# Keys of the first scores in two halves, zero products in every gap of the opening, and new places for three turns

## The chip, the cores and the metric

One core of one Trainium2 chip runs the whole program. The metric is device time in microseconds (us) of one execution, the median of several runs.

## The reference, cut to what matters

```python
B, H, S, D = 4, 8, 768, 48
f = 1.0 / (1.0 + np.exp(-f_logit))
for t in range(S):
    state = f[:, :, t, :, None] * state + np.einsum('bhd,bhe->bhde', k[:, :, t], v[:, :, t])
    y[:, :, t] = np.einsum('bhd,bhde->bhe', q[:, :, t], state)
x = y.transpose(0, 2, 1, 3).reshape(B * S, H * D)          # 3072 x 384
h = x @ w_in                                               # 384 -> 2048
g = np.where(h >= 1, h, np.where(h <= -1, 0.0, (h + 1) ** 2 / 4))
out = g @ w_out                                            # 2048 -> 384
```

All of it is float32. A linear attention with a gate for each head and channel gives the tokens of a two-layer network.

## The kernel before, in words

**Tiling.** The 768 tokens are cut into six steps of 128 (`NI`, `C`). In a step the eight heads are taken in four pairs (`PAIRS`, `NP`), and a pair's operands hold all four batches side by side, 4 x 128 = 512 columns (`N`): keys in the first 512 columns of its tile `kq`, queries in the next 512. Pair 3 of a step is made of rows that are left over from the three tiles of 16 + 96 channels into which the 384 channels of the network are cut; in step 0 it is loaded on its own, in later steps its keys and queries are moved out of the tiles of pairs 0 to 2 (`move`, L295, six small transfers a step). A pair is numbered through all steps, so pair 3 of step 0 is 3, pairs 4 to 7 are those of step 1. In the trace the four tiles are one name, `kq`; in the order of the program kq_67 to kq_70 belong to pairs 0 to 3.

**Step 0, the opening.** For each pair `first_loads` (L444) issues the gate logits (192 KB) and the keys and queries (512 KB) on SP's queue, by `dma` (L292), pair 3 first. ScalarE (ACT) makes log(1 + exp(-logit)) of them in two passes (L455, L456). `first_gates` (L458) sums these over time on TensorE (PE), one product with a triangle of ones for each batch (L465); ACT takes the exponentials of the sums, of either sign (L468, L469), and VectorE (DVE) multiplies keys and queries by them in place (L473, L474). `scores` (L564) are sixteen records of products of keys with queries, L572 (two heads by four batches), masked by DVE (L579, L585). `last_heads` (L808) and `half_tile` (L820) multiply the masked scores with the values (L806) for the tiles of the network's input: "last" is pair 3's share, "heads" of a tile its own pairs' share, and "tile" the products that put pair 3's rows into the tile (L836). Whichever of "heads" and "tile" comes first for a tile opens its bank in PSUM; where that is "heads", a product with zeros clears the bank first (L827). `unit_0` (L853) is the first product with w_in.

**Behind it.** The network runs in 96 units: a step has 16 slices of w_in, w_out (`NJ`). A unit's nine products of x with w_in (L266) are followed by ACT and DVE (L269 to L280) and by nine products with w_out for the unit before (L287). The parts of w_in, w_out are split into high and low halves while they arrive (`split_piece`, lines 362 to 373). Between the units stand the attention's blocks of the next steps: the table `TURNS` (L57) says at which unit a pair is prepared and its keys transposed ("turn", L640, with L642's copies behind it), `VISITS` (L58) at which units two pairs' scores, states and outputs are made. `prepare` issues the pair's loads, gates and moves too.

**What sets the order.** Every operation is given to `Plan` with an engine, a cost in ns (`COST`) and what it needs. TensorE's operations keep the order in which they are added: `START` (L59) for the opening, then the units with their tables. For the other engines and the queues `Plan.order` (L116) runs the list against its own costs and sets one order for each engine, by what is free, ready and due. The program is then written out in that order; it is fixed, and each instruction waits for semaphores of what it needs. A DMA issue on SP that waits holds back all that stand behind it.

**Zero products.** `warm_first` (L335, tuple `WARM`, L61) gives PE 32 products with zeros before the first operands are there. Later, the loop that writes the program out (L1001) puts products of 512 columns with zeros (`warm`, L329, L332) where the plan shows a gap on PE: from 7 to 20 us, gaps over 350 ns, and behind 20 us, those over 500 ns.

## Time and profile before

| | |
|---|---|
| median of three runs | 469.04 us (468.89 to 469.52) |
| the profiled execution | 469.33 us |
| its span in the trace | 467.5 us |
| PE busy in the span | 460.9 us, 99% |
| DVE busy | 346.5 us, 74% |
| ACT busy | 299.4 us, 64% |
| mean traffic | 106 GB/s of HBM over the span |

All times in the trace count from the start of the span; the execution is 1.8 us longer than its span. L12 is line 12 of the kernel. Engines that run beside PE cost nothing as long as PE has work, so a share is read together with the chain of work that ended last and, in a stretch, with the engine's timeline and what released each wait. PE is TensorE's products, PEld its weight loads, POOL is GpSimd, SP the queue that issues nearly all transfers.

### The profile page before, as it was taken

What the parts mean: (1) busy time and instruction counts of PE and PEld (TensorE: products, weight loads), DVE (VectorE), ACT (ScalarE), POOL (GpSimd) and SP (SyncE); (2) the same over time, 40 slices, a digit from 0 to 9 for tenths busy, and PEclk for the clock granted to TensorE, in tenths of its full rate; (3) what the DMA queues carried; (4) which work ended last, traced back from release to release, by engine and by line L of the source; (5) the groups of instructions that cost most, each with busy time, mean ns of one, the idle gap of its engine ahead of it and who ended that gap; (6) DMA issues with size and microseconds to landing.
All of it is one profiled execution on the core that took longest, in us unless ns stands there. A gap on an engine that the chain in (4) does not pass through costs nothing.

```text
span 467.5 us, 11025 instructions
## 1 busy us (share of the span) xinstructions
PE 460.9 (99%) x4525; PEld 378.8 (81%) x4525; DVE 346.5 (74%) x689; ACT 299.4 (64%) x551; POOL 22.6 (5%) x75
## 2 busy tenths in 40 slices
PE   8999999999999999999999999999999999999996
PEld 7887788888888888888888888888888888888884
DVE  2989998789999889989878788566766755533332
ACT  7798998989566776578475546654545454644443
POOL 2202010000000200000020001000000000000000
PEclk9999999999999999999999999999999999999999
DMA  8878685444023333053335323245322224300001
GB/s 271 310 241 257 187 285 181 169 129 145 1 69 126 105 78 102 2 193 109 75 84 193 129 67 91 68 130 127 126 81 70 67 79 126 102 1 0 1 0 71
DMA packets 21861, 54.36 MB, mean 116 GB/s; under 512 B 3568, under 2 KB 4464, under 8 KB 21808
## 3 DMA queue, kind: packets, MB, share of 16 engines
q1 hardware_dynamic: 21664, 53.57, 37.0%
q8 instruction: 36, 0.59, 0.6%
q14 instruction: 17, 0.14, 0.1%
q10 hardware_dynamic: 144, 0.07, 0.1%
HBM read 44.96 MB, written 4.72 MB: 106 GB/s over the span
## 4 chain that ended last, share of the span: by engine, by line
PE 92%; DVE 3%; ACT 2%; DMA 1%; issue 1%; SPq 0%; DVEq 0%; ACTq 0%
PE po L287 41%; PE ph L266 39%; PE pa L688 2%; PE pa L710 2%; PE ph L621 1%; DVE kn L655 1%; DMA raw<-in_l 1%; PE pa L759 1%; PE po L572 1%; PE pa L806 1%; DVE glo L280 1%; PE pa L640 1%; PE ph L860 0%; DVE act L277 0%; PE pa L621 0%
## 5 line engine op out<-in xcount | busy, mean ns | idle before, releaser
L266 PE MATMUL ph<-x,w_hi 128*128 128x512 f32 x570 | 146.5, 389 | 0.0
L269 ACT ACTIVATE act<-ph,half 128x512 f32<-128x512 f32 x96 | 66.1, 689 | 93.2 <-PE ph L266 92.8
L266 PEld LDWEIGHTS ph<-x,w_hi 128*128 128x128 f32 x570 | 106.8, 188 | 22.6 <-ACT w_hi L372 0.4
L277 DVE SCALAR_TENSOR_TENSOR act<-ph,act 128x512 f32<-128x512 f32 x96 | 66.2, 690 | 61.6 <-ACT act L272 60.5
L889 ACT CAST ghi<-act 128x512 fp32r<-128x512 f32 x96 | 59.4, 619 | 51.1 <-DVE act L277 50.5
L287 PE MATMUL po<-ghi,w_hi 128*128 128x512 f32 x288 | 86.3, 401 | 0.0
L287 PE MATMUL po<-ghi,w_lo 128*128 128x512 f32 x288 | 83.2, 390 | 0.0
L287 PE MATMUL po<-glo,w_hi 128*128 128x512 f32 x288 | 82.9, 389 | 0.0
L280 DVE TENSOR_TENSOR glo<-act,ghi 128x512 fp32r<-128x512 f32 x96 | 66.2, 689 | 21.5 <-ACT ghi L889 20.0
L266 PE MATMUL ph<-x,w_lo 128*128 128x512 f32 x285 | 81.7, 389 | 0.0
L655 DVE STREAM_TRANSPOSE kn<-kq 32x128 f32<-32x128 f32 x224 | 67.7, 302 | 3.6
L287 PEld LDWEIGHTS po<-ghi,w_lo 128*128 128x128 f32 x288 | 54.1, 188 | 11.6
L287 PEld LDWEIGHTS po<-glo,w_hi 128*128 128x128 f32 x288 | 54.1, 188 | 11.5
L266 PEld LDWEIGHTS ph<-x,w_lo 128*128 128x128 f32 x285 | 53.5, 188 | 11.1
L272 ACT ACTIVATE act<-act 128x512 f32<-128x512 f32 x96 | 60.7, 632 | 2.9
L287 PEld LDWEIGHTS po<-ghi,w_hi 128*128 128x128 f32 x288 | 51.9, 188 | 11.3 <-ACT ghi L889 0.3
L383 DVE TENSOR_REDUCE ok<-raw 128x1 f32<-128x384 f32 x64 | 33.2, 545 | 2.2 <-DMA raw<-in_w 2.2
L367 ACT ACTIVATE bits<-raw,top_of 128x384 uint32<-128x384 fp8e4 x32 | 20.1, 642 | 1.1 <-DMA raw<-in_w 1.1
L558 ACT ACTIVATE sd<-sd,kq 112x48 f32<-112x48 f32 x80 | 19.2, 324 | 0.0
L373 DVE TENSOR_TENSOR w_lo<-bits,w_hi 128x384 fp32r<-128x384 f32 x32 | 17.6, 554 | 1.9 <-ACT w_hi L372 1.7
L503 DVE TENSOR_TENSOR_SCAN w<-rec,f 128x512 f32<-128x512 f32 x15 | 18.3, 1220 | 0.9 <-ACT f L502 0.8
L369 DVE SCALAR_TENSOR_TENSOR bits<-raw,bits 128x384 uint32<-128x384 uint32 x32 | 17.4, 550 | 0.0
(137 smaller groups left out, 372.5 us busy)
## 6 DMA issues: line engine op xcount, KB each, us to landing
raw<-in_w SPq DMA_DIRECT2D x32, 384.0 KB, 3.1
raw<-in_w SPq DMA_DIRECT2D x32, 383.6 KB, 3.8
kq<-in_kq SPq DMA_DIRECT2D x15, 512.0 KB, 5.0
v<-in_v SPq DMA_DIRECT2D x12, 384.0 KB, 4.6
out_y<-raw SPq DMA_DIRECT2D x18, 256.0 KB, 2.7
f<-in_f SPq DMA_DIRECT2D x15, 256.5 KB, 3.3
kq<-in_k SPq DMA_DIRECT2D x4, 512.0 KB, 7.2
kq<-kq SPq DMA_DIRECT2D x30, 64.2 KB, 3.5
```

Source lines behind the costliest of these rows:

```text
L266: nc.tensor.matmul(ps, w_in(w_hi if high else w_lo, j, kt), xt[:, kt, t], start=(n == 0), stop=(n == 8))
L269: nc.scalar.activation(a, ps, AF.Relu, bias=half, scale=0.5)
L272: nc.scalar.activation(a, a, AF.Square)
L277: nc.vector.scalar_tensor_tensor(out=a, in0=ps, scalar=1.0, in1=a, op0=ALU.max, op1=ALU.min)
L280: nc.vector.tensor_tensor(out=lo, in0=a, in1=hi.bitcast(F32), op=ALU.subtract)
L287: nc.tensor.matmul(po[e], w_out(part, j, e), g, start=(j == 0 and n == 0), stop=(j == NJ - 1 and n == 2))
L367: m = sca("bits", lambda: nc.scalar.activation(t, top, AF.Abs, bias=top_of, scale=2.0 ** 30), loaded, made[k - 4] if k >= 4 else None, set ...
L383: seen.append(vec("join", lambda z=z, op=op: nc.vector.tensor_reduce(out=ok[:, 1 + NG + z + c:2 + NG + z + c], in_=words_of(raw[2])[1].bit ...
L503: s1 = vec("scan", lambda: nc.vector.tensor_tensor_scan(out=wide(w), data0=wide(rec), data1=ft[:, N:0:-1], initial=0.0, op0=ALU.mult, op1= ...
L558: nc.scalar.activation(ds[:, at + b * D:at + (b + 1) * D], state[:, p * B + b], AF.Copy, scale=pf[:R, b:b + 1])
L655: nc.vector.transpose(kn[n % 2][to:to + 32, ::-1, r:r + 32], src[:, :, u:u + 32])
L889: o = g["hi"] = sca("copy", lambda: nc.scalar.copy(hi, a), o, unit_out.get(u - 2))
```

## The change

- The gates and scores of pair 3 in step 0 are made in two halves of two batches: logits, logarithms, sums, exponentials, multiplies and scores each in two (numbers 3 and 7 in `START`).
- The logits of the second half are issued on ACT's queue. Pair 3's keys and queries come in two transfers of 256 KB: the inner columns 256 to 767 (the keys of batches 1 and 0, which lie last, and the queries of batches 0 and 1), then the outer quarters, columns 0 to 255 and 768 to 1023.
- `START` has another order: pair 2's gates go ahead of pair 1's, and for each tile "tile" goes ahead of "heads", for tile 0 too, so that no bank is cleared.
- `WARM` is seven products of 512 columns and two of 256. A new function, `fill`, puts zero products of 256 columns into every planned gap of over 100 ns between 4 and 20 us.
- The planner's figures for the opening's transfers (`KB_FIRST`, `KB_LATER`, `KB_L`) and halves are new, and with them the order of SP, ACT and DVE.
- `TURNS` puts the turns of pairs 5 to 9, 18, 19, 22 and 23 earlier (by one unit, those of 8 and 9 by four). `VISITS` puts the three visits of pairs 4 and 5 one unit earlier, the outputs of pairs 8 and 9 and the three visits of pairs 10 and 11 one unit later.

```diff
+KB_FIRST, KB_LATER, KB_L = 1.75, 0.82, 1.0
+COST = dict(half_gates=460, half_scores=570, half_log=330, half_sig=330, half_gate=350, gates=870,
...
-TURNS = {4: 4, 5: 5, 6: 9, 7: 9, 8: 19, 9: 19, 10: 25, 11: 25, 12: 28, 13: 28, 14: 37, 15: 37, 16: 40, 17: 40, 18: 47, 19: 47, 20: 61, 21: 61, 22: 70, 23: 70}
-VISITS = {4: (5, 6, 7), 6: (10, 12, 13), 8: (21, 22, 25), 10: (25, 26, 28), 12: (28, 32, 37), 14: (37, 39, 40), 16: (40, 46, 47), 18: (47, 60, 61), 20: (61, 69, 70), 22: (70, 75, 77)}
-START = (("gates", 3), ("gates", 0), ("scores", 3), ("mask", 3), ("gates", 1), ("scores", 0), ("mask", 0), ("gates", 2), ("last", 3),
-         ("scores", 1), ("mask", 1), ("heads", 0), ("scores", 2), ("mask", 2), ("tile", 2), ("tile", 1), ("tile", 0), ("heads", 1), ("heads", 2), ("unit", 0), ("unit", 1), ("unit", 2))
-WARM = 28 * (128,) + 4 * (256,)
+TURNS = {4: 4, 5: 4, 6: 8, 7: 8, 8: 15, 9: 15, 10: 25, 11: 25, 12: 28, 13: 28, 14: 37, 15: 37, 16: 40, 17: 40, 18: 46, 19: 46, 20: 61, 21: 61, 22: 69, 23: 69}
+VISITS = {4: (4, 5, 6), 6: (10, 12, 13), 8: (21, 22, 26), 10: (26, 27, 29), 12: (28, 32, 37), 14: (37, 39, 40), 16: (40, 46, 47), 18: (47, 60, 61), 20: (61, 69, 70), 22: (70, 75, 77)}
+START = (("gates", 3), ("gates", 7), ("gates", 0), ("scores", 3), ("scores", 7), ("mask", 3), ("gates", 2), ("gates", 1), ("last", 3),
+         ("scores", 0), ("scores", 1), ("mask", 0), ("tile", 0), ("heads", 0), ("scores", 2), ("mask", 1), ("tile", 1), ("heads", 1), ("mask", 2), ("tile", 2), ("heads", 2), ("unit", 0), ("unit", 1), ("unit", 2))
+WARM = 7 * (512,) + 2 * (256,)
 BY_PRODUCT, ON_EITHER = (), 16
 AFTER = {0: (("turn", 0), ("turn", 1)), 1: (("states", 0),), 2: (("turn", 2), ("turn", 3)), 3: (("states", 2),)}
...
                 nc.tensor.matmul(opened["bank"], zeros, zeros.rearrange("p (o c) -> p o c", o=1).broadcast_to([128, 4, 128]),
                                  start=opened["start"], stop=opened["start"])
+    def fill(gap):
+        for _ in range(int(gap / 115 + 0.5)):
+            nc.tensor.matmul(ph[1][:, 0:256], zeros, zeros.rearrange("p (o c) -> p o c", o=1).broadcast_to([128, 2, 128]), start=True, stop=True)
+
     def warm_first():
         for cols in WARM:
             nc.tensor.matmul(ph[1][:, 0:cols], zeros, zeros[:, 0:128].rearrange("p (o c) -> p o c", o=1).broadcast_to([128, max(cols // 128, 1), 128])[:, :, 0:min(cols, 128)], start=True, stop=True)
...
     cleared = add("POOL", 500, clear)
+    def later_half(n):
+        ends = [a.rearrange("r (o z) -> r o z", o=4)[:, 0:4:3] for a in (kq[n][:, 0:2 * N], kd[n])]
+        return dma(*ends, KB_FIRST * 256)
+
     def first_loads(n):
         c, a = att[n], LOGS[n]
+        raw_l = WEIGHTS[n][1][:, 0:BOTH]
+        c["l"] = []
+        parts = 2 if n == NP - 1 else 1
+        some = [slice(k * B // parts, (k + 1) * B // parts) for k in range(parts)]
+        loads = []
+        for k in range(parts):
+            cols = slice(k * BOTH // parts, (k + 1) * BOTH // parts)
+            if k == 0:
+                loads.append(dma(raw_l[:, cols], ld[n, :, cols], KB_L * 192 / parts))
+            else:
+                loads.append(add("ACT", "issue", lambda cols=cols: nc.scalar.dma_start(raw_l[:, cols], ld[n, :, cols]), kb=KB_L * 192 / parts))
         if n == NP - 1:
             ready["mask"] = add("ACT", "issue", lambda: nc.scalar.dma_start(mask_z, maskd[:, 0:C + 1]), kb=64)
             ready["sel"] = dma(ident, identd, 64)
-        raw_l = WEIGHTS[n][1][:, 0:BOTH]
-        l = dma(raw_l, ld[n], 192)
-        rows = 128
-        c["lk"] = dma(kq[n][:rows, 0:2 * N], kd[n, :rows], 4 * rows)
-
-        e = sca("log", lambda: nc.scalar.activation(spread(a), raw_l.rearrange("t (m h d) -> t m h d", m=B, h=2), AF.Exp, scale=-1.0), l, cleared)
-        c["l"] = sca("log", lambda: nc.scalar.activation(spread(a), spread(a), AF.Ln, bias=one), e, set_consts)
+        mid = slice(N // 2, 3 * N // 2)
+        if parts == 1:
+            c["lk"] = [dma(kq[n][:, 0:2 * N], kd[n], KB_LATER * 512)]
+        else:
+            c["lk"] = [dma(kq[n][:, mid], kd[n, :, mid], KB_FIRST * 256)]
+            c["lk"].append(later_half(n))
+        log = "log" if parts == 1 else "half_log"
+        for m, l in zip(some, loads):
+            e = sca(log, lambda m=m: nc.scalar.activation(spread(a)[:, m], raw_l.rearrange("t (m h d) -> t m h d", m=B, h=2)[:, m], AF.Exp, scale=-1.0), l, cleared)
+            c["l"].append(sca(log, lambda m=m: nc.scalar.activation(spread(a)[:, m], spread(a)[:, m], AF.Ln, bias=one), e, set_consts))
     def first_gates(n):
+        k, n = divmod(n, NP)
         t, c, (kw, qw) = kq[n][:R], att[n], [a[:R] for a in WEIGHTS[n]]
-        _, ps, held = bank((1, 2, 0, 0)[n])
+        parts = len(c["l"])
+        if k == 0:
+            c["ps"] = bank((1, 2, 0, 0)[n])
+            c["was"], c["lf"], c["exp"], c["s2"], c["km"], c["qm"], c["kq"] = list(c["ps"][2]), [], [], [], [], [], []
+        _, ps, held = c["ps"]
+        some = range(k * B // parts, (k + 1) * B // parts)
+        back = slice(N - (k + 1) * N // parts, N - k * N // parts)
+        on = slice(k * N // parts, (k + 1) * N // parts)
+        half = "" if parts == 1 else "half_"
         def sums():
-            for m in range(B):
+            for m in some:
                 nc.tensor.matmul(ps[:R, B - 1 - m], LOGS[n][:, m * C:m * C + R], mask_z[:, 0:C], start=True, stop=True)
-        c["lf"] = o = add("PE", "gates", sums, c["l"], ready["mask"], held)
-        k = sca("sig", lambda: nc.scalar.activation(kw, wide(ps)[:R], AF.Exp, scale=-1.0), o)
-        q = c["s2"] = sca("sig", lambda: nc.scalar.activation(qw, wide(ps)[:R, ::-1], AF.Exp), o)
-        held[:] = c["exp"] = [k, q]
-        c["en"] = add("POOL", "least", lambda: nc.gpsimd.tensor_copy(
-            out=ok[:R, 1 + n * B:1 + n * B + B], in_=kw.rearrange("r (b c) -> r b c", b=B)[:, ::-1, C - 1]), k)
-        c["km"] = vec("gate", lambda: nc.vector.tensor_tensor(out=t[:, 0:N], in0=t[:, 0:N], in1=kw, op=ALU.mult), k, c["lk"])
-        c["qm"] = vec("gate", lambda: nc.vector.tensor_tensor(out=t[:, N:2 * N], in0=t[:, N:2 * N], in1=qw, op=ALU.mult), q, c["lk"])
-        c["kq"] = [c["km"], c["qm"]]
+        c["lf"].append(add("PE", half + "gates", sums, c["l"][k], ready["mask"], c["was"]))
+        o = c["lf"][-1]
+        e = sca(half + "sig", lambda: nc.scalar.activation(kw[:, back], wide(ps)[:R, back], AF.Exp, scale=-1.0), o)
+        q = sca(half + "sig", lambda: nc.scalar.activation(qw[:, on], wide(ps)[:R, ::-1][:, on], AF.Exp), o, c["l"])
+        c["s2"].append(q)
+        c["exp"] += [e, q]
+        held[:] = c["exp"]
+        if k == parts - 1:
+            c["en"] = add("POOL", "least", lambda: nc.gpsimd.tensor_copy(
+                out=ok[:R, 1 + n * B:1 + n * B + B], in_=kw.rearrange("r (b c) -> r b c", b=B)[:, ::-1, C - 1]), c["exp"])
+        c["km"].append(vec(half + "gate", lambda: nc.vector.tensor_tensor(out=t[:, back], in0=t[:, back], in1=kw[:, back], op=ALU.mult), e, c["lk"][k]))
+        c["qm"].append(vec(half + "gate", lambda: nc.vector.tensor_tensor(out=t[:, N:][:, on], in0=t[:, N:][:, on], in1=qw[:, on], op=ALU.mult), q, c["lk"][k]))
+        c["kq"] += [c["km"][-1], c["qm"][-1]]
     def first_decays():
...
         if i == 0:
             first_loads(n)
             if n % 2 == 0:
-                c["lv"] = dma(v[k], vv[0, n // 2], 384)
+                c["lv"] = dma(v[k], vv[0, n // 2], KB_LATER * 384)
             return
         ours = range(NT * i, NT * i + NT) if p == NP - 1 else [NT * i + p]
         for m in ours:
...
     def scores(n):
+        k, n = divmod(n, NP)
         c = att[n]
-        held = [bank(b) for b in ((5, 6), (3, 4), (5, 2), (3, 4))[n]]
+        parts = len(c["l"])
+        if k == 0:
+            c["held"] = [bank(b) for b in ((5, 6), (3, 4), (5, 2), (3, 4))[n]]
+            c["sc"] = []
         def emit():
-            for m in range(B):
-                for (a, z), (_, ps, _) in zip(HEADS, held):
+            for m in range(k * B // parts, (k + 1) * B // parts):
+                for (a, z), (_, ps, _) in zip(HEADS, c["held"]):
                     nc.tensor.matmul(ps[:, m], key(n, m)[a:z], query(n, m)[a:z], start=True, stop=True)
-        c["sc"] = add("PE", "scores", emit, c["kq"], [h[2] for h in held])
-        c["held"] = held
+        c["sc"].append(add("PE", "scores" if parts == 1 else "half_scores", emit, c["kq"][2 * k:2 * k + 2] if parts > 1 else c["kq"], [h[2] for h in c["held"]] if k == 0 else []))
     am_of = [am[2:4], kn, am[0:2], am[0:2]]
...
         for o in plan.order():
             if o.engine == "PE":
                 gap = o.start - idle if idle else 0
-                if 7000 < o.start < 20000 and gap > 350:
-                    warm(int((gap - 100) / 300))
+                if 4000 < o.start < 20000 and gap > 100:
+                    fill(gap)
                 elif o.start > 20000 and gap > 500:
                     warm(int(gap * 0.9 / 230))
                 idle = o.start + o.cost
```

The order of SP's queue in the opening, before (the two `raw` of the first row are the logits of pairs 3 and 0; kq_70 is pair 3's keys and queries, sd the logits of pair 2):

```order
L293 DMA raw<-in_l 128x384 x2
L293 DMA kq_70<-in_k 128x1024
L293 DMA raw<-in_l 128x384
L293 DMA kq_67<-in_k 128x1024
L293 DMA sd<-in_l 128x384
L293 DMA kq_68<-in_k 128x1024
L293 DMA v<-in_v 128x768 [waits DMAHW0_49]
L293 DMA v<-in_v 128x768 [waits DMAHW1_49]
L293 DMA kq_69<-in_k 128x1024 [waits DMAHW2_49]
L293 DMA ident<-in_ident 128x128 [waits DMAHW3_49]
```

and with the change:

```order
L294 DMA raw<-in_l 128x192
L294 DMA raw<-in_l 128x384
L294 DMA kq_70<-in_k 128x512
L294 DMA kq_70<-in_k 128x2x256 [waits DMAHW4_49]
L294 DMA sd<-in_l 128x384
L294 DMA raw<-in_l 128x384
L294 DMA kq_67<-in_k 128x1024 [waits DMAHW0_49]
L294 DMA v<-in_v 128x768 [waits DMAHW1_49]
L294 DMA kq_68<-in_k 128x1024 [waits DMAHW2_49]
L294 DMA ident<-in_ident 128x128 [waits DMAHW3_49]
L294 DMA kq_69<-in_k 128x1024
```

The second transfer into kq_70 stands behind a wait for semaphore DMAHW4, which belongs to the first one. The logits of pairs 2 and 1, all other keys and the values are issued behind it.

The order of DVE in the same place, before (L473 and L474 multiply pair 3's keys and queries, then pair 0's):

```order
L473 TENSOR_TENSOR kq_70<-kq_70,raw 112x512 [waits DMAHW3_49,Activation_49]
L474 TENSOR_TENSOR kq_70<-kq_70,raw 112x512 [waits DMAHW1_49,Activation_49]
L473 TENSOR_TENSOR kq_67<-kq_67,raw 112x512 [waits DMAHW5_49,Activation_49]
L474 TENSOR_TENSOR kq_67<-kq_67,raw 112x512 [waits DMAHW2_49,Activation_49]
L585 TENSOR_TENSOR am_75<-po_114,mask 128x512 [waits DMAHW0_49,PE_49]
```

and with the change:

```order
L509 TENSOR_TENSOR kq_70<-kq_70,raw 112x256 [waits DMAHW5_49,DMAHW4_49,Activation_49]
L510 TENSOR_TENSOR kq_70<-kq_70,raw 112x256 [waits DMAHW1_49,DMAHW0_49,Activation_49]
L509 TENSOR_TENSOR kq_70<-kq_70,raw 112x256 [waits Activation_49]
L510 TENSOR_TENSOR kq_70<-kq_70,raw 112x256 [waits Activation_49]
L624 TENSOR_TENSOR am_75<-po_114,mask 128x512 [waits DMAHW2_49,PE_49]
L624 TENSOR_TENSOR am_76<-po_115,mask 128x512 [waits PE_49]
```

Four multiplies of 256 columns stand for the two of 512. The first waits for two transfers' semaphores, DMAHW5 and DMAHW4, and the masks of pair 3's scores (L585, now L624) are ahead of pair 0's multiplies.

The order of PE with the change, from the second half of pair 3's scores (L612) over pair 2's sums (L497, act_83) to pair 1's (f_66); before, pair 1's sums stood right behind the scores:

```order
L612 MATMUL po_114<-kq_70 128x128 [waits DMAHW5_49,DVE_49]
L612 MATMUL po_115<-kq_70 128x128
L612 MATMUL po_114<-kq_70 128x128
L338 LDWEIGHTS zeros
L338 MATMUL ph_113<-zeros 128x256
L497 MATMUL pa_109<-mask,act_83 112x128 [waits Activation_49]
L497 MATMUL pa_109<-mask,act_83 112x128 x3
L497 MATMUL pa_111<-mask,f_66 112x128 [waits Activation_49]
L497 MATMUL pa_111<-mask,f_66 112x128 x3
```

A row that repeats is shown once: between the scores and pair 2's sums stand three products of `fill` (L338), and one between pair 2's and pair 1's. Further back three stand ahead of pair 1's scores and two ahead of pair 2's, nine in all.

## Rows read from the trace of the kernel before

**Rows 1.** The page's busy time of each engine, share of the span, instructions.
```profile
PE 460.9 (99%) x4525; PEld 378.8 (81%) x4525; DVE 346.5 (74%) x689; ACT 299.4 (64%) x551; POOL 22.6 (5%) x75
```

**Rows 2.** Chain that ended last, the opening: start us, duration us, engine or transfer, line.
```profile
1.29 0.42 SPq L293
...
2.23 5.72 DMA raw<-in_l
...
7.97 0.53 ACT f L455
...
8.53 0.61 ACT f L456
...
12.18 1.06 PE pa L465 x8
...
14.24 1.09 PE po L572 x16
...
15.34 0.32 PE pa L827
...
21.23 2.28 PE ph L860 x9
```

**Rows 3.** Timeline of PE, opening: start us, us, engine, line, operation, out<-in, xcount [idle].
```profile
5.00 1.48 PE L465 MATMUL pa<-mask,act 128*112 128x128 f32 x8
...
6.31 1.04 PE L465 MATMUL pa<-mask,f 128*112 128x128 f32 x8
...
8.56 1.16 PE L572 MATMUL po<-kq 48*128 48x128 f32 x16 [0.35 <-DVE kq L474]
...
9.65 1.13 PE L465 MATMUL pa<-mask,f 128*112 128x128 f32 x8
...
11.01 0.37 PE L572 MATMUL po<-kq 48*128 48x128 f32 x1 [0.23 <-DVE kq L474]
```

**Rows 4.** Chain that ended last, 20 to 120 us.
```profile
44.34 0.45 PE po L332 x2
```

**Rows 5.** Timeline of PE near 69 us; transfers issued at 63.79 (KB, us to landing).
```profile
69.32 0.58 PE L640 MATMUL pa<-ident,kq 112*128 112x112 f32 x4 [0.52 <-DVE glo L280]
...
kq<-kq SPq DMA_DIRECT2D x1, 64.2 KB, 5.3
```

**Rows 6.** Windows: stretch, us, busy PE PEld DVE ACT POOL, clock, DMA share, GB/s.
```profile
12.00:14.00 2.00, 2.00 (x28) 1.75 (x24) 2.00 (x5) 0.88 (x3) 0.07 (x1) 1.00 1.05 386
...
40.00:60.00 20.00, 20.00 (x329) 15.61 (x327) 19.03 (x34) 18.22 (x40) 3.27 (x6) 1.00 0.67 197
```

**Rows 7.** Timeline of DVE, opening.
```profile
7.19 0.72 DVE L473 TENSOR_TENSOR kq<-kq,raw 112x512 f32<-112x512 f32 x1 [6.17 <-ACT raw L468]
...
7.83 0.68 DVE L474 TENSOR_TENSOR kq<-kq,raw 112x512 f32<-112x512 f32 x1
...
19.26 0.54 DVE L373 TENSOR_TENSOR w_lo<-bits,w_hi 128x384 fp32r<-128x384 f32 x1
```

**Rows 8.** Loads issued at 1.29 and 1.75, and at 23.5: KB, us to landing.
```profile
raw<-in_l SPq DMA_DIRECT2D x1, 192.0 KB, 2.9
...
kq<-in_k SPq DMA_DIRECT2D x1, 512.0 KB, 5.3
...
raw<-in_w SPq DMA_DIRECT2D x1, 383.6 KB, 2.9
```

**Rows 9.** Timeline of SP's queue (issues and the waits in them).
```profile
1.75 0.43 SPq L293 DMA_DIRECT2D kq<-in_k  x1
...
7.10 0.33 SPq L293 DMA_DIRECT2D ident<-in_ident  x1
...
7.97 0.33 SPq L293 DMA_DIRECT2D mask_t<-in_mask  x1
```

**Rows 10.** Windows at the end (the granted clock is third from last).
```profile
463.30:466.00 2.70, 0.00 (x0) 0.00 (x0) 0.00 (x0) 0.49 (x1) 0.00 (x0) 1.00 0.78 297
...
466.60:467.50 0.90, 0.00 (x0) 0.00 (x0) 0.00 (x0) 0.00 (x0) 0.00 (x0) 0.50 0.00 0
```

More of the change, by code (lines that the diff above doesn't have):

```diff
@@ L46 @@
 NG = (NP + (NI - 1) * NT) * B
-SMALL_PRODUCTS = ("gates", "scores", "heads", "own", "tile", "both", "begin", "before", "part", "states", "parts", "half", "turn")
+SMALL_PRODUCTS = ("gates", "scores", "heads", "own", "tile", "both", "begin", "before", "part", "states", "parts", "half", "turn", "half_gates", "half_scores")
 HOP, LANDING, PER_KB, NEAR, ADDING, PATIENCE, FLAG_BY = 200, 2200, 3.0, 3500, 1500, 0, 60000
-COST = dict(gates=870, log=500, mm=227, scores=1100, heads=950, own=1200, tile=680, both=1090, begin=480, before=930, part=560, states=850, parts=830, turn=350, first=110, last=95,
+KB_FIRST, KB_LATER, KB_L = 1.75, 0.82, 1.0
@@ L53 @@
+COST = dict(half_gates=460, half_scores=570, half_log=330, half_sig=330, half_gate=350, gates=870, log=500, mm=227, scores=1100, heads=950, own=1200, tile=680, both=1090, begin=480, before=930, part=560, states=850, parts=830, turn=350, first=110, last=95,
             rows=316, scan=1140, dve=602, small=200, half=490, sums=467, gate=600, act=575, bits=520, join=465, part_hi=440, cast_384=330, cast=400, round=485, copy=520, turned=412, sig=538, decay=226,
             issue=480, near=600, least=300)
-TURNS = {4: 4, 5: 5, 6: 9, 7: 9, 8: 19, 9: 19, 10: 25, 11: 25, 12: 28, 13: 28, 14: 37, 15: 37, 16: 40, 17: 40, 18: 47, 19: 47, 20: 61, 21: 61, 22: 70, 23: 70}
```

## Prediction

> **What bounds the kernel now.** I read the page's busy shares first, then the chain of work that ended last, then the opening engine by engine. TensorE (PE) is busy 460.9 of 467.5 us [rows 1], so there is little to win outside the places where PE waits. The chain says where these are: it begins with a load, runs over ScalarE (ACT) and VectorE (DVE), and from 11.01 on it is PE, block behind block [rows 2, 3]: gates of four products 1.06 us, scores 1.09, the bank's clearing 0.32, unit 0 at 21.23. So the opening is PE's work from 11.01 on, and what lies ahead of that is waiting. Behind it I find two places that are not work of the reference: two zero products at 44.34 (0.45 us) and a wait of 0.52 us before the second turn at 69.32 [rows 4, 5]. DVE is the other full engine there: 19.03 of 20 us between 40 and 60 [rows 6].
>
> Ahead of 11.01, the scores of pair 3 start at 8.56, behind DVE's two multiplies, the first at 7.19 [rows 3, 7]. They need pair 3's keys, issued at 1.75 and 5.3 us under way, so there at 7.1 [rows 8, 9]. The other thing to see is in SP's queue: the identity's load is issued at 7.10 and mask_t's at 7.97, the moments at which the keys and pair 1's gates (2.23 + 5.72 = 7.95) land [rows 2, 9]. An issue that waits for a landing holds the whole queue until then.
>
> **The change, part by part.**
>
> *The two transfers of keys.* The order of SP shows that the second transfer waits for the semaphore of the first (DMAHW4), and the order of DVE that its first multiply waits for both (DMAHW5 and DMAHW4). The second transfer writes the outer quarters, whose hull holds the inner ones. So the halves do not overlap: the second is issued when the first has landed, and no multiply starts before the second has. Everything behind it on SP (gates of pairs 2 and 1, keys of pairs 0, 1, 2, both values) stands still too.
>
> First half: pair 0's gates, now ahead of it, were issued at 1.29 and took 2.9, so landed at 4.2 [rows 2, 8]. The whole transfer then took until 7.1, 512 KB in 2.9 us or 177 KB/us; at that rate 256 KB land at 5.65. At the 386 KB/us of 12 to 14 us [rows 6] it would be 4.9. I take 5.4, nearer to the row of the same tile at the same time. Second half: a load of 384 KB on a quiet queue takes 2.9 us from issue, one of 192 KB in the opening also 2.9 [rows 8]. I take 2.9, so 8.3. Bounds: 0.3 less for the missing 128 KB at 386 KB/us, 0.4 more because it is 256 rows of 1 KB; together with the first half's bounds, 7.5 to 8.95.
>
> The Trainium skill, DMA: Bandwidth & Descriptors, section "Anatomy of one DMA", gives a transfer a fixed 2.0 us and bytes at 436 GB/s on top, for loads issued from another engine than here; that speaks against cutting one transfer into two that follow each other. As an estimate by that page the second half would take 2.6 us instead of 2.9, and the sum below would be 0.3 less.
>
> *DVE.* A multiply of 512 columns takes 0.72 and one of 384 takes 0.54 [rows 7], so one of 256 some 0.4, and they start 0.32 apart, half of the 0.64 between the starts of the two before. From 8.3 the four halves end at 8.3 + 3 x 0.32 + 0.4 = 9.7. The scores of the second half (0.55, half of 1.09) end at 10.3; before, the scores ended at 9.65, where the next block starts [rows 3]. **+0.65**.
>
> *ACT.* The two half gates, the second issue ahead of the table load and the four half exponentials are hidden: they are due when the keys land, at 8.3, and the exponentials started at about 6.5 before, behind sums that began at 5.00 [rows 3]. The order lets the first of them wait for all four sums, so they start a few tenths later, by 7; the cover is 1.3 us. If the keys came at 7.5 it would still be 0.5. The shorter warming (4096 columns for 4608) ends sooner than the first sums can start and costs nothing.
>
> *PE from there on.* From 9.65 to 21.23 the trace has 11.58 us: blocks that the change only reorders, the clearing (0.32), which goes, since tile 0 now opens its bank, and a wait before 11.01 (11.01 less 9.65 less 1.06, 0.30). That goes as well if each block's inputs are there. With 386 KB/us after 8.3: gates of pairs 2 and 1 land at 8.8 and 9.3, their logarithms take 1.2 each [rows 2], so their sums can start at 10.0 and 11.1, and PE comes to them at 10.6 and 11.8. Keys of pair 0 land at 10.6 (PE needs the products at 13.9), pair 1 at 12.9 (15.3), pair 2 at 14.4 (18.1). All in time, so -0.62.
>
> *Zeros.* Behind the scores of pair 3 the order has nine products of 256 columns: three ahead of the gates of pair 2, one, three ahead of the scores of pair 1, two ahead of those of pair 2. Where the planner saw a gap there is none now, since PE is late and everything else is ready; they are on the path. Two of 512 took 0.45 [rows 4], so 0.11 each: **+1.0**. Those ahead of 9 us lie in waiting time and cost nothing. The opening is therefore 0.65 - 0.62 + 1.0 = 1.0 us longer, and unit 0 starts at 22.2 or 22.3.
>
> *Places.* The two products at 44.34 are gone: **-0.45**. For this, the turn of pair 5 is due in unit 4 with that of pair 4, and their scores right behind it, on a DVE that is full there [rows 6]. What would be late is the multiplied keys of pair 5. No row shows it; below lies nothing, above some 0.9, and the wait of 0.52 before a turn [rows 5] is the nearest: I take **+0.3**. The second turn itself is put a unit earlier, and the moves into pair 7's keys (5.3 us from issue [rows 5]) with it: its wait stays, 0, between -0.5 and +0.5. Turns and visits moved later in the kernel fall among blocks that leave no gap, and cost nothing.
>
> **The sum**: 1.0 - 0.45 + 0.3 = +0.85. The profiled execution took 469.33 (span 467.5 and 1.8 around it), 0.3 above the median of 469.04; the difference goes onto the median: **469.9 us**. By the bounds of the key landing alone it is 469.1 to 470.5.
>
> **Rivals.**
>
> *The keys come early and the second turn stops waiting* (faster). The second half lands at 7.5 and the opening grows by 0.2 only; the products at 44.34 go (-0.45); the moves, issued a unit earlier, have landed when PE comes to the turn (-0.5 of idle, -0.2 of restart). That is 468.1. For it: the 386 KB/us of 12 to 14 us, if the opening ran at that rate; against it: the keys' own row and the order, in which moves and turn go forward together. It decides where the moves are issued over 0.7 us earlier against PE than now. 0.14.
>
> *The halves cost little* (no change). As before, but the turn waits on: 468.8. 0.11.
>
> *DVE is late in units 4 to 8* (slower). Pair 5's multiplies, 1.4 us with DVE full, push the masks and the MLP's steps behind them; 0.9 more, 470.8. For it the 95% between 40 and 60, against it that PE waits nowhere there now. 0.11.
>
> *The clock falls* (slower). PE would be without work from about 7.9 to 9.0, longer than any gap of the trace before its end. The granted clock is 1.00, the 2.4 GHz level, between 463.3 and 466 although PE has nothing to do, and 0.50, 1.2 GHz, from 466.6 on [rows 10]; so a wait of 2.7 us did not lower it, which speaks against. If it did, eight sums at the start took 1.48 against 1.04 right behind [rows 3], so some 4.5 us of blocks would take 2 more: 472. 0.07.
>
> The Trainium skill, TensorE: Matmul & The Clock Gate, section "What's actually happening", has the clock follow how busy the array has been; by that rule the fewer zeros between 8 and 9 us are a risk.
>
> **Chances.** 0.57 for the forecast with its spread of 469.1 to 470.8, which 0.2% (0.94 us, about what a measurement of this kernel can tell from no change) cuts in half at 470.0; 0.14, 0.11, 0.11 and 0.07 for the rivals. Slower: 0.29 + 0.11 + 0.07 = 0.47. Same: 0.28 + 0.11 = 0.39. Faster: 0.14. The range that leaves out the clock and the far halves of the first and third rival is 468.2 to 471.2.
>
> **What would show it.** SP issues the second transfer at about 5.4, when the first lands, and nothing between; DVE's first multiply starts at 8.3, the moment of the second landing, and not at 7.2; PE runs without gap from about 9.8; unit 0 starts at 22.2; no zeros near 44; PE waits by some tenths in unit 4. I am wrong if the second transfer goes out at about 2.3, if DVE starts at 7.2, if the zeros behind the scores stand in idle time, or if the wait before the second turn is gone.

## The result, and the profile after

The change took **474.01 us** (median of six, 472.85 to 475.12) against 469.28 beside it: 1.0093 times the kernel before, 95% interval 1.0064 to 1.0121. By that ratio it is some 4.4 us slower (the two medians lie 4.7 apart); the forecast was 469.9, slower by 0.85, in 468.2 to 471.2. The profiled execution took 474.95 us with a span of 473.1; before, 469.33 and 467.5. A second profiled execution of the same program, told of below, took 473.12.

PE's busy time, the first view, hardly answers: it rose by 2 us and the span by 5.5 [rows 1].

```profile
span 473.1 us, 11001 instructions
...
PE 463.0 (98%) x4514; PEld 378.5 (80%) x4514; DVE 346.0 (73%) x690; ACT 299.6 (63%) x556; POOL 23.2 (5%) x75
```

PE's waits in the whole execution (what it waited for: us in total, times, longest) give the places to look at:

```profile
PE pa L679 <- DMA raw<-in_w: 1.1, 1, 1.1
PE ph L342 <- DVE zeros L307: 1.1, 1, 1.1
PE po L612 <- DVE kq L510: 1.0, 1, 1.0
PE pa L497 <- ACT f L479: 0.7, 1, 0.7
PE ph L798 <- DVE kn L694: 0.4, 1, 0.4
```

**The opening, SP first.** SP's timeline, from the second transfer of keys on, and that transfer's time to landing:

```profile
5.27 0.39 SPq L294 DMA_DIRECT2D kq<-in_k  x1
5.70 0.47 SPq L294 DMA_DIRECT2D sd<-in_l  x1
6.21 0.43 SPq L294 DMA_DIRECT2D raw<-in_l  x1
6.69 0.43 SPq L294 DMA_DIRECT2D kq<-in_k  x1
...
kq<-in_k SPq DMA_DIRECT2D x1, 256.0 KB, 3.2
```

It goes out at 5.27 and lands at 8.46; pair 2's logits, pair 1's and the keys of pair 0 follow at 5.70, 6.21 and 6.69 (before, SP had issued all three loads of that kind by 3.6). The windows of the same stretch say what this did to the stream of loads (columns as in [rows 6]); the second fence is the kernel before:

```profile
5.00:6.00 1.00, 1.00 (x7) 0.88 (x6) 0.00 (x0) 0.70 (x2) 0.00 (x0) 1.00 0.00 0
6.00:8.00 2.00, 2.00 (x16) 1.93 (x15) 0.00 (x0) 0.73 (x3) 0.00 (x0) 1.00 0.78 175
8.00:10.00 2.00, 1.03 (x12) 0.66 (x10) 1.41 (x4) 1.96 (x5) 0.91 (x3) 1.00 0.98 310
10.00:11.00 1.00, 1.00 (x14) 0.64 (x10) 0.02 (x1) 0.14 (x1) 0.00 (x0) 1.00 0.68 144
```

```profile
5.00:6.00 1.00, 1.00 (x7) 1.00 (x7) 0.00 (x0) 0.97 (x2) 0.00 (x0) 1.00 0.86 249
6.00:8.00 2.00, 2.00 (x17) 1.47 (x15) 0.81 (x2) 1.12 (x4) 0.19 (x1) 1.00 0.91 314
8.00:10.00 2.00, 1.65 (x20) 1.32 (x20) 0.84 (x2) 1.97 (x4) 0.31 (x1) 1.00 1.03 396
10.00:11.00 1.00, 0.78 (x8) 0.58 (x6) 1.00 (x3) 0.97 (x3) 0.40 (x1) 1.00 1.03 412
```

Between 5 and 6 nothing moves, where 249 GB/s moved before, and up to 11 the rate stays behind. DVE's timeline shows who waits for it: its multiplies of pair 3, then the first of pair 0 and of pair 1, each of the last two released by a landing. Before, pair 0's began at 9.66 and was released by ACT.

```profile
8.59 0.42 DVE L509 TENSOR_TENSOR kq<-kq,raw 112x256 f32<-112x256 f32 x1 [7.58 <-ACT raw L502]
...
9.60 0.42 DVE L510 TENSOR_TENSOR kq<-kq,raw 112x256 f32<-112x256 f32 x1
...
13.31 0.69 DVE L509 TENSOR_TENSOR kq<-kq,raw 112x512 f32<-112x512 f32 x1 [0.91 <-DMA kq<-in_k]
...
15.59 0.69 DVE L509 TENSOR_TENSOR kq<-kq,raw 112x512 f32<-112x512 f32 x1 [0.98 <-DMA kq<-in_k]
```

PE's timeline, which answers to [rows 3]:

```profile
9.40 0.71 PE L612 MATMUL po<-kq 48*128 48x128 f32 x8 [0.97 <-DVE kq L510]
10.05 0.39 PE L338 MATMUL ph<-zeros 128*128 128x256 bf16 x2
10.37 0.71 PE L612 MATMUL po<-kq 48*128 48x128 f32 x8
11.02 0.50 PE L338 MATMUL ph<-zeros 128*128 128x256 bf16 x3
...
13.18 1.13 PE L497 MATMUL pa<-mask,f 128*112 128x128 f32 x8 [0.68 <-ACT f L479]
...
24.52 0.50 PE L899 MATMUL ph<-x,w_lo 128*128 128x512 f32 x1
```

Pair 3's scores end at 11.02 instead of 9.65, and unit 0 starts at 24.52, where the same timeline has 21.16 before (21.23 in the chain of [rows 2]): the opening is **3.4 us** longer. Of that, 1.37 us are there when the scores end; from there to unit 0 PE takes 13.50 us instead of 11.51. On this way it waits once, 0.68 us for pair 1's logarithms. For the late keys of pairs 0 and 1 it shows no wait: other blocks and zeros fill that time.

**Behind the opening.** The zeros at 44 are gone. The second turn (L679, which answers to L640 of [rows 5]) waits 1.11 us at 68.15 instead of 0.52. In the second profile it doesn't wait at all, so this wait is not the change's. Another wait is new, in unit 46, where the products of states wait for four of DVE's transposes; before, this block took 0.83 us without a wait, here 1.50. The last two lines are DVE's first transposes of pair 18, with the change and before:

```profile
68.15 0.57 PE L679 MATMUL pa<-ident,kq 112*128 112x112 f32 x4 [1.11 <-DMA raw<-in_w]
...
248.14 0.24 PE L798 MATMUL ph<-v,kn 64*48 64x48 f32 x1 [0.36 <-DVE kn L694]
...
246.83 1.26 DVE L694 STREAM_TRANSPOSE kn<-kq 32x128 f32<-32x128 f32 x4
...
249.15 0.92 DVE L655 STREAM_TRANSPOSE kn<-kq 32x128 f32<-32x128 f32 x3
```

The tables explain it, and it is more than a matter of time. With the change the turns of pairs 18 and 19 stand in unit 46, as the states of pairs 16 and 17 do, and within a unit the program lists turns first. Pairs 16 and 18 use the same buffer, `kn[0]`. So these transposes write keys of pair 18 into it, and the products for pair 16 wait for them and read what they wrote; before, the products (from 244.21) were through when they began. The turns of pairs 22 and 23 (unit 69) stand ahead of the states of pairs 20 and 21 in the same way, without a wait that shows. In both places the change doesn't compute quite what the kernel before does.

**The end.** PE's last product ends at 467.26 instead of 463.16, 4.10 later, but the span is 5.5 longer. The last output store lands at 470.06; from there to the end it takes 2.99 us, before 1.47. SP's instructions in the trace there, times in us:

```
                                              before    change
last output store lands                       466.07    470.06
  on which of the eight DMA semaphores        7th       1st
SP's last branch begins                       464.20    468.60
SP's next instruction, 1st semaphore's wait   464.72    471.09
SP's wait for the 7th semaphore               466.08    471.58
span ends                                     467.54    473.05
```

The program ends with SP waiting for the eight semaphores in their order. The change has two loads more, so the last store signals the first semaphore, and six waits that used to pass while it was under way come behind it. And SP stands 2.4 us behind its branch instead of 0.45, 1.0 of them after the landing.

### The profile page after: what moved, and what is told of

It is laid out like the page before. It is cut to its first block, busy times and chain, and to the rows that moved or that the text cites. A ratio compares the mean times of both kernels' runs of the same rounds, so it can differ in the third digit from the quotient of the medians.

```text
span 473.1 us, 11001 instructions
## 1 busy us (share of the span) xinstructions
PE 463.0 (98%) x4514; PEld 378.5 (80%) x4514; DVE 346.0 (73%) x690; ACT 299.6 (63%) x556; POOL 23.2 (5%) x75
## 5 line engine op out<-in xcount | busy, mean ns | idle before, releaser
L543 POOL COPY end<-w 128x4 f32<-128x4 f32 x15 | 5.5, 368 | 260.8 <-ACT w L542 260.8
```

## The experiments

Times are medians; the ratio is to the kernel before on the same chip, with its 95% interval, and runs on different chips are compared by it. Of most runs there is one profile. "Unit 0" is the start of its first product in PE's timeline (21.16 before, 24.52 and, in the second profile, 23.84 in the change), "PE's end" that of its last product. The opening falls into two parts, pair 3's scores and PE's way from the next block to unit 0. In PE's timeline, in us:

```
                          scores start   next block   unit 0   way to unit 0
kernel before                 8.56           9.65      21.16       11.51
change                        9.40          11.02      24.52       13.50
change, second profile        9.43          11.05      23.84       12.79
e_three                       8.24           9.86      22.21       12.35
e_nofill                      9.35          10.66      23.50       12.84
e_three_nofill                7.21           8.78      21.45       12.67
b_hold                       10.12          11.21      24.02       12.81
b_p47                         9.25          10.34      21.55       11.21
b_p47, second profile         8.82           9.91      21.12       11.21
b_p47_rot8                    8.28           9.37      20.59       11.22
mended                        7.26           8.83      22.10       13.27
```

**Nothing waits in SP's queue** (`e_three`):

```diff
-            c["lk"].append(later_half(n))
+            c["lk"].append([dma(kq[n][:, cols], kd[n, :, cols], KB_FIRST * 128)
+                            for cols in (slice(0, N // 2), slice(3 * N // 2, 2 * N))])
```

> The change, but the outer quarters of pair 3's keys come in two transfers of 128 KB, each in columns of its own, so that no transfer waits for another; SP's order behind them is as in the change. Theory A (the wait of the second transfer in SP's queue holds all loads behind it, and their lateness makes the opening long): all three are issued by 3.1 us, the last lands by about 6.5, the keys of pairs 0 and 1 land at 9.5 to 11 and 11.5 to 13 instead of 13.22 and 15.50, unit 0 starts at 21.5 to 22.3 instead of 24.52, the time falls by 2 to 3 us against the change, to 471 to 472. Rival B (the zeros and the halves of PE make it long): unit 0 still starts at 24 or later, 473.5 or more. Rival C (the new places of turns and visits carry the loss): the time stays at 474.

471.49 us, 1.0056 (1.0041 to 1.007). SP issues all three transfers in one stretch:

```profile
1.76 1.38 SPq L294 DMA_DIRECT2D kq<-in_k  x3
3.19 0.43 SPq L294 DMA_DIRECT2D sd<-in_l  x1
```

The last lands at 6.58, the keys of pairs 0 and 1 at 10.76 and 13.04, unit 0 starts at 22.21. A of the three theories holds: of the 3.4 us of the opening 2.3 are the wait (1.6 against the second profile). Some 1.2 of that lie at the first scores, which end at 9.86 instead of 11.02 or 11.05. Behind them PE's way is shorter by 1.15 us, or by 0.44 against the second profile: that much the later loads cost. PE waits for nothing on this way in `e_three`, and it is still 0.84 longer than before: by the zeros and the blocks of "tile" in PE's timeline.

**The wait alone, in the kernel before** (`b_hold`): pair 3's keys in the two transfers of the change, all else as it was.

```diff
-        c["lk"] = dma(kq[n][:rows, 0:2 * N], kd[n, :rows], 4 * rows)
+        if n == NP - 1:
+            mid = slice(N // 2, 3 * N // 2)
+            ends = [a.rearrange("r (o z) -> r o z", o=4)[:, 0:4:3] for a in (kq[n][:, 0:2 * N], kd[n])]
+            c["lk"] = [dma(kq[n][:, mid], kd[n, :, mid], 256), dma(*ends, 256)]
+        else:
+            c["lk"] = dma(kq[n][:rows, 0:2 * N], kd[n, :rows], 4 * rows)
```

> The kernel before, with pair 3's keys in the two transfers of the change and nothing else. Theory A: the second transfer is issued at about 5.3, lands at 8.4, the keys of pair 0 at 12 to 13, unit 0 starts at 22.8 to 23.8 instead of 21.23, the time is 470.9 to 471.9. Forecast's step (only the first scores are late, later loads arrive in time): unit 0 at 21.6 to 22, 469.6 to 470. Rival C: 469.3.

472.27 us, 1.0071 (1.0048 to 1.0094); unit 0 at 24.02. The opening is 2.9 us longer here, nearly as much as the change's, and longer than expected, because of a second thing: PE waited 1.99 us ahead of the first scores, and some 1.4 us after it began again the granted clock fell to 0.50, the 1.2 GHz level, for 3.4 us. PE's timeline and the windows (the clock is third from last):

```profile
10.12 1.16 PE L577 MATMUL po<-kq 48*128 48x128 f32 x16 [1.99 <-DVE kq L479]
11.21 1.84 PE L470 MATMUL pa<-mask,f 128*112 128x128 f32 x8
...
14.96 1.13 PE L470 MATMUL pa<-mask,act 128*112 128x128 f32 x8
...
8.00:11.40 3.40, 1.41 (x18) 1.17 (x18) 1.49 (x3) 2.11 (x4) 0.19 (x1) 1.00 1.01 309
11.50:14.80 3.30, 3.30 (x24) 3.01 (x22) 3.29 (x6) 2.22 (x4) 0.71 (x1) 0.50 1.00 399
14.90:20.00 5.10, 5.10 (x67) 4.19 (x67) 4.64 (x9) 3.59 (x8) 2.70 (x10) 1.00 1.04 397
```

Eight sums took 1.84 us there instead of 1.04 to 1.13 [rows 3]. That is the rival of the clock, in a kernel where the wait was long. Of the 2.9 us, 1.56 are there when the scores end, and the other 1.30 lie in the stretch at half clock: from pair 2's sums on, at 14.96, where the clock is back, PE needs 9.06 us to unit 0, and before it needed 9.05 from the same block at 12.11. So `b_hold` shows no cost of the later loads. The six runs agree with the clock's part: three with a mean granted clock of 0.999 to 1.000 took 470.31, 471.04 and 472.56 us, the other three (0.993 to 0.995, the profiled one among them) 472.08, 472.45 and 473.73.

**No zeros** (`e_nofill`, `e_three_nofill`): in the change, and in the run with three transfers,

```diff
-                if 4000 < o.start < 20000 and gap > 100:
-                    fill(gap)
-                elif o.start > 20000 and gap > 500:
+                if o.start > 20000 and gap > 500:
```

> The change without any zero product behind the first warming. Theory A: most of the zeros stand where PE would wait for late loads anyway; only the two between pair 3's scores and the three behind them (0.32 and 0.34 us) are on the path, so unit 0 starts 0.3 to 0.7 earlier than 24.52, and the time is 473.3 to 473.8. Rival B (the nine zeros are all on the path): unit 0 starts 1.0 to 1.5 earlier, 472.5 to 473. Rival D (the zeros keep the clock up): the granted clock falls in a stretch of the opening and the time rises by 1 us or more.

> The change with the keys' outer quarters in two transfers (nothing waits in SP's queue) and without zeros behind the first warming. Theory A: with the loads early again PE is the bound and the zeros are on its path: unit 0 starts at 20.9 to 21.6 instead of 22.21, the time falls by 0.6 to 1.3 us against the run with three transfers, to 470.2 to 470.9. Rival (zeros hidden here too): unit 0 at 22.2, 471.5. Rival D (clock): a stretch at half clock in the opening, 472 or more.

In the change 474.07 us, 1.0122 (1.0104 to 1.014), no gain; unit 0 at 23.50, earlier by 1.02 than in the first profile of the change and by 0.34 than in the second. With three transfers 470.92, 1.0033 (1.0022 to 1.0043); unit 0 at 21.45 instead of 22.21, PE's end 0.93 earlier. So the zeros cost 0.6 to 1.1 us (medians, unit 0, PE's end, ratios) when the loads are there. But it isn't the nine behind the scores that cost this. Without zeros the block behind the scores starts 1.08 us earlier, and PE's way from there is 0.32 longer, since it now waits 0.78 us on it for ACT and DVE. What was saved are the zeros ahead of and between the two halves. In the change PE waits ahead of the scores with or without zeros, and no gain shows in the time. No stretch of half clock came with their absence in either profile, but the rival of the clock isn't excluded in the change: two of the four runs of `e_nofill` have a mean clock of 0.989 and 0.995 (475.06 and 474.17 us), the other two 0.998 and 0.997 (473.13 and 473.97).

**The old places in the change** (`e_places`: `TURNS` and `VISITS` as before) **and the new ones in the kernel before** (`b_places`):

> The change with the turns and visits of the kernel before. Theory A: the opening stays (unit 0 at about 24.5) and what comes behind it costs what it costs in the kernel before: the later part of the trace gives back 0.8 us, 473.2. Forecast: the new places are worth 0.15 to 0.45 us, so the old ones make it 474.2 to 474.5. Rival C (the loss is in the places): 470 to 471.

> The kernel before with the turns and visits of the change and nothing else. Theory G (the zeros at 44 us go, but the turn of pairs 18 and 19 a unit earlier than before makes the products of states in unit 45 wait for VectorE's transposes, 0.67 us in the trace of the change): PE's end moves by -0.2 to +0.3 us, and a wait of 0.3 to 0.4 us ahead of the second states product shows near 244 us; the time is 468.7 to 469.4. Forecast's step: -0.15 to -0.45 and no wait in the later part. Rival C: the places alone cost 1 us or more.

474.40 us, 1.011 (1.0093 to 1.0128), and 469.39, 0.999 (0.9971 to 1.0009): in the kernel before, the places as a whole do nothing that can be measured. The profile of `e_places` had a stretch of half clock too (11.25 to 14.66, unit 0 at 24.94), behind a wait of 2.07 us, with a mean clock of 0.996 over the execution. Of its five runs the only one with 0.998 is the fastest, 472.76, so `e_places` doesn't settle what the places are worth in the change. In `b_places` the second part of theory G stands in the trace: from unit 33 to unit 46 PE is 1.2 us ahead of the kernel before, and 0.4 from unit 47 to the end.

**That one turn put back** (`b_p47`: in `b_places`, `18: 47, 19: 47`):

> The kernel before with the new turns and visits, but pairs 18 and 19 turned at unit 47 as before. Theory G (that turn alone costs 0.7 to 0.8 us, the other places give some 0.4 to 1.0): no wait of the states products near 244 us, PE's end 0.9 to 1.3 us ahead of the kernel before, time 468.0 to 468.7, that is 0.6 to 0.8 less than with all new places. Rival (the wait has another cause): the wait stays, 469.4.

The wait is gone from the trace and PE's end is 0.74 us earlier than before (1.43 in a second profile). The time is 469.37 all the same, 1.0 (0.9987 to 1.0013): a miss of the expected time by 0.8. What PE gained was lost at the end: the last store lands 3.26 us behind PE's end (before 2.91), and from there it takes 1.99 us, as SP stands 2.13 us behind its branch, though the last store is on the seventh semaphore as before.

**The order of the semaphores at the end** (`a_rot6`: in the change, six transfers of 4 bytes while SP is idle, `b_rot2`: two in the kernel before):

```diff
+    spare = const.tile([1, 8], F32, name="spare")
+    for k in range(6):
+        move(spare[:, k:k + 1], one[0:1], unit_out[NI * NJ - 12])
     for u in range(NI * NJ - 3, NI * NJ):
```

> The change, with six transfers of 4 bytes on SP's queue near the end, where it is idle, so that the last output store signals the seventh of the eight DMA semaphores again, as in the kernel before, and not the first. Theory E (the end of the program waits for the eight semaphores in their order, and with the last store on the first one, all the other waits come behind its landing): the stretch from PE's last product to the end of the span falls from 5.8 us to 4.3 to 4.6, the time to 472.5 to 473. Rival F (the longer end comes from the code, or from chance): the stretch stays at 5.5 or more, 474.

> The kernel before, with two transfers of 4 bytes on SP's queue near the end, so that the last output store signals the first of the eight DMA semaphores, as in the change. Theory E: the stretch from PE's last product to the end grows from 4.4 us to 5.0 to 5.8, and the time by 0.6 to 1.4, to 469.5 to 470.3. Rival F: 4.4 and no change.

The change fell to 472.59 us, 1.0064 (1.0048 to 1.0079), with 1.47 us from the last landing to the end; SP stood 0.45 us. The kernel before rose to 470.25, 1.0021 (1.0007 to 1.0034), with 1.95. So by the traces the first semaphore costs 0.5 us, and in the change the long stand of SP another 1.0. The times go the same way, though the intervals of the change and of `a_rot6` overlap.

**Is the stand the program's?** (`after_again` and `b_p47_again`: the same kernels once more; `b_p47_rot8`: `b_p47` with eight such transfers, which leave the order of the semaphores and add instructions)

> The change once more, unaltered, for a second profile. If the long stand of SP behind its last branch belongs to the program, it is there again: 2.2 to 2.5 us, and 5.6 to 5.9 us from PE's last product to the end. If it belongs to the execution, 4.9 to 5.1. The hold is there again (second transfer issued at 5.2 to 5.5, landing at 8.3 to 8.6); pair 1's logits land at 9.4 to 10.6 if their lag was chance, at 11.9 if not.

> The run with all new places but one, once more, unaltered, for a second profile. Program: SP stands 2.2 us behind its branch again and the end takes 5.1 to 5.3 us. Execution: 0.5 us and 4.4.

> The run with all new places but one, and eight transfers of 4 bytes near the end: the last store is on the seventh semaphore as before, but the instructions behind it lie elsewhere. If the long stand belongs to the place of the instructions, it is gone or at least other than in that run: with 0.5 us the end takes 4.4 to 4.7 and the time is 468.4 to 468.8, that is 0.6 to 0.9 less. If it does not depend on that, the end stays at 5.2 and the time at 469.3.

SP stood 2.40 us in the change again (2.42 the first time), 2.35 in `b_p47` (2.13), and 0.45 in `b_p47_rot8`. So it belongs to the program and not to the execution, and eight more transfers remove it; that it is the place of the instructions is not shown, since the transfers do other things too. The time is 468.15 us, **0.9974** (0.9962 to 0.9986), the lowest of all, though the turns of pairs 22 and 23 still stand ahead of the states of pairs 20 and 21 here. The end is no shorter in its profile, against the expectation: 1.48 us from the landing on, but the last store lands 3.93 us behind PE's end (3.26 and 3.40 in `b_p47`), 5.4 us together where 4.4 to 4.7 was expected. What is shorter is the time up to the first scores: they start at 8.28, in `b_p47` at 9.25 and 8.82, and from the next block on PE takes 11.2 us to unit 0 in all three. So this one profile doesn't explain the gain of the median.

What SP waits for in the stand is open. In `b_p47` it ends 0.05 and 0.08 us behind the last landing, in the change 1.0 us behind it. The traces have two transfers of the instruction queue in the stand, of 8 KB each, but there are two as well just behind the short stand of `b_p47_rot8`, so this doesn't tell.

In the second profile of the change the second transfer went out at 5.36 and landed at 8.48; pair 1's logits landed at 9.51, not at 11.94. In the first profile two of their sixteen parts came 2.4 us behind the others: that differs from execution to execution, and it explains the 0.7 us between the two openings.

**Tile 0 first** (`b_p47_tile`; `b_p47_tile_rot8` with the eight transfers):

```diff
-         ("scores", 1), ("mask", 1), ("heads", 0), ("scores", 2), ("mask", 2), ("tile", 2), ("tile", 1), ("tile", 0), ("heads", 1), ...
+         ("scores", 1), ("mask", 1), ("tile", 0), ("heads", 0), ("scores", 2), ("mask", 2), ("tile", 2), ("tile", 1), ("heads", 1), ...
```

> As the run with all new places but the turn of pairs 18 and 19, and tile 0's products with pair 3's rows ahead of its own heads, so that no bank is cleared. Expected: 0.3 us less for the clearing if nothing waits (467.7 to 468.4); rival: the identity's rows or pair 3's rounded output are late there, PE waits 0.3 us or more ahead of them, and nothing is won (468.0 to 469).

> As the run before it, with tile 0's products with pair 3's rows first (no bank cleared). PE's end 1.0 to 1.1 us ahead of the kernel before. With the short stand of SP 468.1 to 468.6, the fastest of all; with the long one 469.0 to 469.5.

469.51 us, 1.0 (0.9987 to 1.0013), a miss of the hoped-for 467.7 to 468.4, and 468.43, 0.9987 (0.9976 to 0.9999): nothing won over the same kernels without it. The clearing's 0.32 us goes, but the planner puts a zero product of 0.25 there, and the products of "tile" take 1.75 in two blocks instead of 1.59 in one.

**Four things undone in the change** (`mended`: three transfers, no zeros, that turn at 47, five transfers at the end):

> The change with four things undone: the keys' outer quarters in two transfers, no zeros behind the first warming, the turn of pairs 18 and 19 at unit 47 again, and five transfers of 4 bytes near the end that put the last store on the seventh semaphore. Theory (the four are what the change lost): against the run with three transfers and no zeros (470.9) 0.6 to 0.8 less for the turn and 0.6 to 0.9 less for the end, so 469.2 to 469.7, the time of the kernel before, with unit 0 at 21.4. Rival (the halves or the remaining places lose more): 470.3 or more. Rival (the halves gain after all): 468.5 or less.

469.72 us, 1.001 (0.9999 to 1.0021): as expected, the time of the kernel before within about 0.1%. But unit 0 is at 22.10 and not at 21.4. PE's way to it shows what the halves do: the first scores start 1.3 us earlier than before, and PE then waits 1.5 us, 0.18 for logarithms, 0.80 for a load of values and 0.51 for pair 1's multiplied queries: things that the halves do not bring earlier by as much. Against `b_p47_rot8`, which has the same places and the short stand, `mended` is slower by 0.36% by the ratios. So what is left of the change in the opening doesn't pay, and the return to the old time has a gain in it, that of the other places.

## Why the prediction was wrong

It was right that it is slower, and about the mechanism at the first scores; it missed 3.5 of 4.4 us. Three steps failed: the first scores were priced too low, "all in time" was wrong, and the end was put at nothing.

- **The two transfers**: right. Issued at 5.27 (forecast 5.4), landed at 8.46 (8.3), DVE's first multiply at 8.59, the last ended at 10.02 (9.7). The estimate by the figures of the Trainium skill for the second half (DMA: Bandwidth & Descriptors, "Anatomy of one DMA") was 2.6 us; the trace has 3.2, and decides. The 0.4 us that its upper bound allows for rows of 1 KB had no row behind it.
- **The first scores, +0.65: a term too small.** +1.37, and +1.40 in the second profile. From the start of the first half at 9.40 PE takes 0.65, 0.32 for two zeros that were not in the sum, and 0.65; I had put a half at 0.55 and let only the second count.
- **"All in time, so -0.62": the step that failed.** I let the loads run at 386 KB/us from 8.3 on, and each be there when PE comes. The chip moved 144 GB/s between 10 and 11, and the keys of pairs 0 and 1 landed at 13.22 and 15.50 (12.42 and 14.82 the second time), not at 10.6 and 12.9. By the sum, PE's way from the scores to unit 0 was 11.96 us (11.58 - 0.62 + 1.0; the 11.58 is 0.07 too long, as it takes 21.23 from the chain and 9.65 from the timeline, which has 21.16); it took 13.50 and 12.79. `e_three` parts this: where no transfer waits, the way is 12.35, so the later loads cost 1.15 and 0.44 us. The remaining 0.4 is no matter of loads: the clearing's 0.32 was no gain, as "tile" in three blocks of 0.66 us takes 1.98 instead of 1.59, and the nine zeros take 1.2 us in `e_three`, 0.43 for three of them and 0.32 for two.
- **Zeros, +1.0**: the size looks right (0.6 to 1.1 in `e_three_nofill`), but by luck. That run gains ahead of and between the two halves of the scores, where the sum had nothing, and not behind them, where it had the nine.
- **Places**: no zeros near 44, right; DVE late in unit 4 (+0.3), wrong, no wait is there; the second turn's wait grew in one profile and was gone in the other; "moved later cost nothing", wrong: pairs 18 and 19 a unit earlier cost 0.7 to 0.8 us (`b_p47`).
- **The end: put at nothing, +1.4.** From PE's end to the end of the span it took 5.79 and 5.77 us in the two profiles, before 4.38. I counted the two added transfers only where they are issued. Each moves all later ones to the next semaphore, and with `a_rot6` most of this came back.
- **The rivals**: the keys didn't come early, and the halves' cost was not little. The clock did not fall in either profile of the change (1.00 from 7 us to the end of PE's work), but it did in two relatives with waits of 2 us. The slowest of the six runs, 475.12 us, has a mean clock of 0.994 where the others have 0.997 to 0.999; about that is what `b_hold`'s profile has with its 3.4 us at 0.50 (0.995). So the rival was probably there in one run of six, and 0.07 was not too high. What I held against it was weak: at the end of the kernel before the clock did fall, later in the same idle stretch [rows 10], and in `b_hold` it fell when PE was at work again.

Added up, the first profile has 3.36 us more in the opening, 0.74 from unit 0 to PE's end and 1.42 at the end: the 5.5 us of the span. The second has 2.68, 0.38 less and 1.40: 3.7 us. The median lies between.

## What to carry to other kernels

When an issue waits in a queue that feeds everything, price the hole in the stream: shift every load behind it, and check each consumer, the first with all that stands on its engine, then those behind it. A first consumer that is served earlier gains nothing if the loads of the next ones come no earlier, as `mended` shows. Here two writes into one tile whose column ranges interleave were put one behind the other, and three contiguous pieces were not; that the outer bounds decide is how I read it. Before an operation that writes a buffer is moved in a table, look for who still reads it. Count DMAs to the end of the program: the semaphore of the last store and the stand of SP behind its last branch were worth 1.5 us here.

## What I had not expected of the hardware

- From the last landing to the end of the span it took 1.41 to 1.48 us with the last store on the seventh or eighth semaphore and a short stand of SP, 1.95 with the first, 1.86 and 1.97 with the second and a stand of 2.1 us, 1.99 to 2.03 with the seventh and a stand of 2.1 to 2.4, and 2.91 to 2.99 with the first and a stand of 2.4.
- After PE had waited 2.0 us the granted clock fell to 0.50 for 3.4 us in two profiles, 1.4 and 2.0 us after PE had begun again, but not in the profile of `e_nofill`, where PE had waited 2.5, nor in the second profile of the change, with 1.7. What decides is open.
- The same opening ended up to 1.0 us apart in different executions. In `b_p47`, `b_p47_again` and `b_p47_rot8` the difference was there when the first scores started; in the change two of the sixteen parts of a transfer came 2.4 us behind the others.
